# Prefix sums of a step: on GpSimd while no batch is in the pipe, on VectorE otherwise (graph message passing, one core)

## The chip, the core and the metric

The kernel runs on one core of one Trainium2 chip. The metric is the device time of one execution in microseconds (us). TensorE (PE) multiplies, its weight loads are listed as PEld, VectorE is DVE, ScalarE is ACT, GpSimd is POOL, and SyncE (SP) issues plain DMAs. GpSimd issues the indirect DMAs.

## The reference

One layer of message passing over a graph of 12,500 nodes and 800,000 edges, 64 features a node and 16 an edge, float32:

```
def reference(x, e_attr, src, dst, w_msg, w_upd):
    N, D = x.shape
    m_in = jnp.concatenate([x[src], x[dst], e_attr], axis=-1)
    msg = _silu(m_in @ w_msg)
    agg = _segment_sum(msg, dst, N)
    return _silu(jnp.concatenate([x, agg], axis=-1) @ w_upd)
```

`src` and `dst` are random, so the edges have to be sorted by target before they can be summed.

## The kernel before

The nodes are cut into 128 buckets of 98 nodes. Two streams of work run beside one another.

**Steps** sort edges. There are 782 of them. A step takes 8 columns of 128 edges. `onehot` (ScalarE, lines 394 and 395) makes `hf`, for every edge the one-hot row of its bucket. `sums` (lines 401 to 408) makes `G`, prefix sums of these rows over groups of four columns: a copy on ScalarE and two or three adds of 128x256 and 128x128 elements, in the steps of the first part of the kernel always three (403, 403, 405), each of which reads what the one before wrote. `count` (TensorE, 421 to 424) multiplies `hf` and `G` with triangular and ones matrices into `z`, from which `ranks` (VectorE, 429) takes every edge's place within its bucket. `expand` (VectorE, 438 to 442) puts the edge's record at that place in a wide row `X`, one of two buffers; its input `cb` is in PSUM. `move` (TensorE, 459) multiplies `hf` by `X`, which sends every record to its bucket's partition; ScalarE copies the result to `blk` (464, two buffers), `place` (VectorE, 477 and 478) moves the buckets' pointers on, and `scatter` (GpSimd, 482) writes the block to the store in DRAM.

**Batches** use sorted edges. A group of up to 64 tiles is formed over several periods: small VectorE work (lines 540 to 558, 588 and 589), loads of the tiles by SyncE (`rt<-st`, 564), and the conversion of the indices (525). A batch of a group is at most 8 tiles: `gather` of the source nodes' terms (GpSimd, an indirect DMA a tile, 645), one-hot rows, transposes, products, the message (677, 678), and the sum by target (694, 706).

The program is unrolled by hand: `period` writes one step and one batch in a fixed order, each at another stage of its pipe. `h` is the step that enters, `z` the one before it, `s` a block to be scattered; `q`, `t`, `a` and `r` are batches, `q` the one that enters. Each engine works through its instructions in the order in which they were written. `sums` of the entering step stands at one of two places: ahead of `expand` when a batch is in the pipe as `q`, `t` or `a`, behind `expand` when none is. A group is only formed when enough edges are sure to be sorted, by a count of steps, so that the kernel begins with 26 steps without a batch; three more come between the first groups, after which there is always a batch. In the first 20 steps the node tables are made as well (lines 193 to 209; at first four in a step, later one).

Of the kernel before, what the change touches and what calls it, by code (L numbers as in the profile page):

```python
# [7 lines left out]
OP = mybir.AluOpType  # L8
# [40 lines left out]
def mpnn_kernel(tc, x, e_attr, src, dst, w_msg, w_upd, out):  # L49
    nc = tc.nc  # L50
# [22 lines left out]
    with es:  # L73
# [303 lines left out]
        class Step:  # L377
# [16 lines left out]
                    nc.scalar.activation(c.hf[:, k, :], iof, AF.Square, bias=c.hi[:, k:k + 1])  # L394
                nc.scalar.activation(c.hf, c.hf, AF.Relu, bias=ones, scale=-1.0)  # L395

            def sums(c):

                c.G = tp.tile([P, 2, ZB, NBK], BF16, name="G")
                h = c.hf.rearrange("p (a k) b -> p a k b", k=ZB)  # L400
                nc.scalar.activation(c.G[:, :, 0, :], h[:, :, 0, :], AF.Copy)
                for k in (1, 2):
                    nc.vector.tensor_tensor(out=c.G[:, :, k, :], in0=h[:, :, 0, :] if k == 1 else c.G[:, :, k - 1, :], in1=h[:, :, k, :], op=OP.add)  # L403
                a, b = ((0, 2), (1, 2), (0, 1), (0, 1))[c.turn]
                nc.vector.tensor_tensor(out=c.G[:, a:b, 3, :], in0=c.G[:, a:b, 2, :], in1=h[:, a:b, 3, :], op=OP.add)
                if c.turn in (0, 2):
                    a = 1 if c.turn == 0 else 0
                    nc.vector.tensor_tensor(out=c.G[:, a, 3, :], in0=c.before(a), in1=c.G[:, a, 3, :], op=OP.add)

            def before(c, a):  # L410

# [299 lines left out]
        def period(step=None, batch=None, ptr_new=None):  # L711

            h, z, p, s = step, pipe["h"], pipe["z"], pipe["s"]
            q, t, a, r = batch, pipe["q"], pipe["t"], pipe["a"]
            forms = [g for g in work["forming"] if not g.ready()]
            e = None
            pipe.update(h=h, z=z, q=q, t=t, a=a)
            if q:
                q.gather(0, BT // 2)
            if s:  # L720
                s.scatter()
            if q:
                q.gather(BT // 2, BT)
            if h:
                h.onehot()
            if q:
                q.onehot()
            for g in forms:
                g.fourth()
            if z:  # L730
                z.count()
            if t:
                t.transpose(0)
                t.weights()
                t.transpose(1)
            if r:
                r.reduce()
            if z:
                z.ranks()
            if a:  # L740
                a.message()
            if r:
                r.add()
            early = q or t or a
            if h and early:
                h.sums()
            if z:
                z.expand()
            if h and not early:
                h.sums()  # L750
            if p:
                e = p.move(0)
            if t:
                t.product()
            if p:
                p.move(1)
            if e:
                e.place(ptr_new)
            for g in forms:
                g.middle()  # L760
                g.fifth()
            pipe["s"] = e
            return r
# [4 lines left out]
        class Draws:  # L768
# [34 lines left out]
            def take(d, u, units):  # L803
                for f, done in zip(d.free(u), d.done):
                    left = units
                    for b in range(NB):
                        n = min(f[b], left)
                        done[b] += n
                        left -= n
# [48 lines left out]
        def step():  # L858
            c = None
            if flow["ic"] < len(steps):  # L860
                c = next_step(flow["ic"])
                flow["ic"] += 1
            pn = None
            if pipe["z"] and pipe["z"].last:
                if flow["npl"] % 64 == 0:
                    flow["ptrs"] = sg.tile([NBK, 64], I32, name="ptrs")
                pn = flow["ptrs"][:, flow["npl"] % 64:flow["npl"] % 64 + 1]
                flow["npl"] += 1
            b = take()
            if size() and may_start() and draws.holds(state["u"], size() // state["u"]):  # L870
                draws.take(state["u"], size() // state["u"])
                g = stages[state["stage"]]
                start_group(state["u"], state["ptr"], size(), cap=g["cap"], bt=g["bt"])
            elif not size() and (not work["forming"] or work["forming"][-1].k >= 2):
                larger_from()
            if pipe["z"]:
                for i in pipe["z"].last.values():
                    draws.place(Chunk(i).m)
            period(c, b, pn)
# [35 lines left out]
        while pipe["s"]:  # L915
            period(None, take())
# [21 lines left out]
        while work["used"] < large or (work["forming"] and work["forming"][-1].k < 2):  # L938
            b = take()
            if work["used"] < large and may_start():  # L940
                start_group(QU, ptrg)
            period(None, b)
            next(upd, None)
            next(upd, None)
# [61 lines left out]
        while work["used"] < whole or lasts or work["cur"] is not None or work["forming"]:  # L1006
            b = take()
# [47 lines left out]
        with tc.If(more > 0):  # L1055
# [4 lines left out]
            with tc.If(nover > 0):  # L1060
# [27 lines left out]
                with tc.For_i(0, nover, 1):  # L1088
# [29 lines left out]
                    halves = [Step(hi[:, 0:M], rec[:, 0:M, :], 0), Step(hi[:, M:2 * M], rec[:, M:2 * M, :], 1, C - M)]  # L1118
                    for c in halves:
                        c.onehot()  # L1120
                        c.sums()
                        c.count()
                        c.ranks()

                    def block(rs=None):
                        for c in halves:
                            c.expand(rs)
                            e = c.move()
                        return e


                    c = block()
# [4 lines left out]
                    with tc.For_i(0, rounds, 1):  # L1137
                        c = block(rs)
# [36 lines left out]
```

## Time and the profile before

| | |
|---|---|
| Time before, median of 3 runs | 8929.77 us (8925.74 to 8931.5) |
| The profiled execution's own time | 8929.85 us |
| Its span in the profile | 8928.0 us |
| Busy: PE, DVE, ACT, POOL | 8156.2, 7216.6, 5054.3, 6599.6 us |
| First gather issued | 203.42 us from the span's start |

The profile shows one execution. In a row of the timeline the first number is the start in us from the span's start, then the duration, the engine, the line and the operation; what stands in brackets is the idle time of the engine before it and what ended it. In a row by line, the numbers behind the bar are the sum in us and the mean in ns, then the idle time before. TensorE's durations overlap, so starts are compared there. A row merged of several instructions has their count behind an x, and a row of the waits gives the sum of the waits in us, their number and the longest.

### The profile page before, as it was taken

Reading aid. Unit: us, or ns where it says so; the run is one execution under the profiler, and the core shown is the slowest. Engines: PE = TensorE matmul, PEld = TensorE weight load, DVE = VectorE, ACT = ScalarE, POOL = GpSimd, SP = SyncE. Lnnn points to the kernel's source line nnn. Section 1 sums busy time; section 2 is a strip of 40 time slices with the busy share of each in tenths; the row PEclk is TensorE's granted clock in tenths of the full one; section 3 lists DMA queues with packets and bytes.
Section 4 is the critical chain, followed back from the end, with each engine's and each line's share of the span. In section 5 each row is a group of like instructions: output and inputs, shape, how many; then the busy total and the mean of one; then the engine's idle time right before and its main releaser. Section 6 shows DMA issues by size and latency. Waiting matters only on the chain. (4 is left out here: it accounts for less than half of the span.)

```text
span 8928.0 us, 155380 instructions
## 1 busy us (share of the span) xinstructions
PE 8156.2 (91%) x49053; PEld 5873.2 (66%) x49816; DVE 7216.6 (81%) x15722; ACT 5054.3 (57%) x12594; POOL 6599.6 (74%) x6908
## 2 busy tenths in 40 slices
PE   8899999999999999999999999999999999999767
PEld 5677776666666666666666666666666666666656
DVE  8999998888888888888888888888888888887233
ACT  7666666555555555555555555555555555555222
POOL 1677777777777777777777777777777777777776
PEclk9999999999999999999999999999999999999566
DMA  4222222222222222222222222222222222222323
GB/s 109 56 62 60 60 61 58 50 57 54 54 56 50 57 52 56 52 56 52 56 52 56 56 52 52 55 57 52 56 52 56 52 56 55 52 57 49 59 48 51
DMA packets 662901, 501.14 MB, mean 56 GB/s; under 512 B 492983, under 2 KB 529911, under 8 KB 662071
## 3 DMA queue, kind: packets, MB, share of 16 engines
q0 software_dynamic: 238976, 349.72, 16.8%
q1 hardware_dynamic: 422775, 141.27, 7.3%
q8 instruction: 401, 6.57, 0.3%
q14 instruction: 429, 3.51, 0.1%
q10 hardware_dynamic: 320, 0.07, 0.0%
HBM read 330.05 MB, written 152.30 MB: 54 GB/s over the span
## 5 line engine op out<-in xcount | busy, mean ns | idle before, releaser
L645 POOL DMA_INDIRECT g<-A_d,sidx x6322 | 6020.1, 952 | 1946.6 <-issue 1546.2
L459 PE MATMUL pl<-X,hf 128*128 128x291 f32 (+5 forms) x12512 | 4255.3, 492 | 6.2 <-DVE LOST L477 6.2
L459 PEld LDWEIGHTS pl<-X,hf 128*128 128x128 f32 x12512 | 2389.5, 198 | 1333.1 <-issue 842.5
L442 DVE TENSOR_TENSOR X<-cb,rec 128x442 f32<-128x442 f32 (+5 forms) x3128 | 2646.9, 908 | 26.7
L394 ACT ACTIVATE hf<-iof,shi 128x128 f32<-128x128 f32 x6256 | 1908.3, 389 | 872.9 <-PE pl L459 872.6
L673 PEld LDWEIGHTS pre<-w,qt 114*128 114x128 f32 x10496 | 1338.1, 202 | 580.7 <-issue 562.8
L673 PE MATMUL pre<-w,qt 114*128 114x64 f32 x10496 | 1343.6, 284 | 249.0 <-DVE g L677 247.3
L677 DVE TENSOR_TENSOR g<-pre,g 128x512 f32<-128x512 f32 (+1 forms) x818 | 548.9, 671 | 1191.7 <-DMA g<-A_d,sidx 769.4
L678 ACT ACTIVATE g<-g 128x512 f32<-128x512 f32 (+1 forms) x818 | 501.6, 613 | 1761.5 <-DVE g L677 1759.7
L694 PE MATMUL ag<-q,g 128*64 128x98 f32 x12644 | 775.8, 264 | 250.4 <-DVE wl L549 146.1
L429 DVE TENSOR_REDUCE rank<-z 128x8 f32<-128x1024 f32 x782 | 949.1, 1214 | 57.3 <-PE z L424 36.3
L395 ACT ACTIVATE hf<-hf,ones 128x1024 f32<-128x1024 f32 x782 | 899.1, 1150 | 25.4
L667 ACT ACTIVATE qt<-tq 114x1024 f32<-114x1024 f32 (+1 forms) x818 | 797.2, 975 | 156.5 <-PE tq L664 154.2
L664 PE MATMUL tq<-ident,q 128*114 128x128 f32 x6322 | 871.5, 283 | 14.3 <-ACT nodes L194 13.0
L694 PEld LDWEIGHTS ag<-q,g 128*64 128x64 f32 x12644 | 613.3, 143 | 411.5 <-issue 200.6
L664 PEld LDWEIGHTS tq<-ident,q 128*114 128x114 f32 x6322 | 766.9, 140 | 136.5 <-ACT nodes L194 20.5
L482 POOL DMA_INDIRECT st<-blk,ptrs x567 | 572.9, 1010 | 321.2 <-issue 141.1
L655 DVE TENSOR_TENSOR q<-cb,lo 128x784 f32<-128x784 f32 (+1 forms) x818 | 767.4, 938 | 2.2
L464 ACT ACTIVATE blk<-pl 128x512 f32<-128x512 f32 (+1 forms) x568 | 323.8, 570 | 782.9 <-PE pl L459 609.7
L706 DVE TENSOR_TENSOR ACC<-ag,ACC 64x98 f32 x1938 | 497.5, 257 | 108.6 <-PE ag L694 28.8
L422 PE MATMUL z<-G,onesb 128*128 128x384 bf16 x1564 | 511.4, 327 | 73.5 <-DVE G L403 13.7
L673 PE MATMUL pre<-BW,qt 114*128 (+1 forms) x2148 | 311.8, 305 | 109.4 <-DVE g L677 108.6
(137 smaller groups left out, 5099.1 us busy)
## 6 DMA issues: line engine op xcount, KB each, us to landing
g<-A_d,sidx POOLq DMA_INDIRECT x6322
ea<-in_e_attr SPq DMA_DIRECT2D x260, 192.0 KB
rt<-st SPq DMA_DIRECT2D x1312, 34.0 KB
st<-blk,ptrs POOLq DMA_INDIRECT x567
rt<-st SPq DMA_DIRECT2D x434, 8.5 KB
nodes<-in_x SPq DMA_DIRECT2D x62, 98.0 KB
ACC<-rt SPq DMA_DIRECT2D x11, 544.0 KB
rt<-st SPq DMA_DIRECT2D x320, 17.0 KB
```

The costliest lines, as they stand in the source:

```text
L394: nc.scalar.activation(c.hf[:, k, :], iof, AF.Square, bias=c.hi[:, k:k + 1])
L395: nc.scalar.activation(c.hf, c.hf, AF.Relu, bias=ones, scale=-1.0)
L429: nc.vector.tensor_reduce(out=c.rank, in_=c.z, axis=AX.X, op=OP.max)
L442: nc.vector.tensor_tensor(out=c.x[:, k:k + 2, 2:2 + n * R].rearrange("p k (s c) -> p k s c", c=R), in0=hit[:, k:k + 2, 0:n, None].to_broad ...
L459: nc.tensor.matmul(pl[:, 0:w], c.hf[:, k, :], c.x[:, k, 0:w], start=(n == (c.size - 1 if whole else 0)), stop=ends, skip_group_check=True)
L482: i = nc.gpsimd.indirect_dma_start(out=st, out_offset=bass.IndirectOffsetOnAxis(ap=c.ptr, axis=0), in_=c.blk[:, 2:], in_offset=None)
L645: j = nc.gpsimd.indirect_dma_start(out=t.g[:, i, :], out_offset=None, in_=A_d, in_offset=bass.IndirectOffsetOnAxis(ap=t.grp.sidx[:, k:k + ...
L655: nc.vector.tensor_tensor(out=t.q[:, 0:n, 0:BK], in0=ioB[:, None, 0:BK].to_broadcast([P, n, BK]), in1=t.grp.lo[:, i0:i0 + n, None].to_broa ...
L664: nc.tensor.transpose(t.tq[0:KQ, j * P:(j + 1) * P], t.q[:, j, :], ident)
L667: nc.scalar.activation(t.qt[:, 0:w], t.tq[0:KQ, 0:w], AF.Copy)
L673: nc.tensor.matmul(t.pre[:, i * D:(i + 1) * D], t.qt[:, i * P:(i + 1) * P], w, start=True, stop=True)
L694: o = nc.tensor.matmul(t.ag[t.half(v), v // 2 * BK:(v // 2 + 1) * BK], t.g[:, i, :], t.q[:, i, 0:BK], start=(k == 0), stop=(k == u - 1))
```

## The change

`sums` gets the engine of its adds as an argument. Where it stands ahead of `expand` (a batch is in the pipe), and in the rare path at the end for overfull chunks, the adds stay on VectorE. Where it stands behind `expand` (no batch in the pipe), they are written for GpSimd.

```
-            def sums(c):
+            def sums(c, engine):
...
                 nc.scalar.activation(c.G[:, :, 0, :], h[:, :, 0, :], AF.Copy)
                 for k in (1, 2):
-                    nc.vector.tensor_tensor(out=c.G[:, :, k, :], in0=h[:, :, 0, :] if k == 1 else c.G[:, :, k - 1, :], in1=h[:, :, k, :], op=OP.add)
+                    engine.tensor_tensor(out=c.G[:, :, k, :], in0=h[:, :, 0, :] if k == 1 else c.G[:, :, k - 1, :], in1=h[:, :, k, :], op=OP.add)
                 a, b = ((0, 2), (1, 2), (0, 1), (0, 1))[c.turn]
-                nc.vector.tensor_tensor(out=c.G[:, a:b, 3, :], in0=c.G[:, a:b, 2, :], in1=h[:, a:b, 3, :], op=OP.add)
+                engine.tensor_tensor(out=c.G[:, a:b, 3, :], in0=c.G[:, a:b, 2, :], in1=h[:, a:b, 3, :], op=OP.add)
...
             early = q or t or a
             if h and early:
-                h.sums()
+                h.sums(nc.vector)
             if z:
                 z.expand()
             if h and not early:
-                h.sums()
+                h.sums(nc.gpsimd)
```

It moves 87 instructions, three in each of 29 steps. On VectorE, in the steps ahead of the first batch, before and after (`G` is the tile of prefix sums, `X` the wide row, `LOST` and `ptrs` the pointers' work):

```order
 L442 TENSOR_TENSOR X0_183<-cb_139,rec_238 128x2x357
 L442 TENSOR_TENSOR X0_183<-cb_139,rec_238 128x2x408
-L403 TENSOR_TENSOR G_323<-hf_299 128x2x128
-L403 TENSOR_TENSOR G_323<-G_323,hf_299 128x2x128
-L405 TENSOR_TENSOR G_323<-G_323,hf_299 128x128
 L273 SCALAR_TENSOR_TENSOR rec_385<-slo_234,ssi_171 128x24
 L429 TENSOR_REDUCE rank_405<-z_399 128x8
```

The three adds behind the products of `X` are gone, and the next rank follows at once. On GpSimd, at the first blocks that are scattered (`st` is the store), before:

```order
L340 MEMSET done0_153 128x1
L482 DMA st_82<-blk_427,ptr0_149 2938112x17
L482 DMA st_82<-blk_519,ptrs_388 2938112x17
L482 DMA st_82<-blk_614,ptrs_388 2938112x17
L482 DMA st_82<-blk_677,ptrs_388 2938112x17
```

and after, at the same place:

```order
L482 DMA st_82<-blk_427,ptr0_149 2938112x17
L403 TENSOR_TENSOR G_505<-hf_481 128x2x128
L403 TENSOR_TENSOR G_505<-G_505,hf_481 128x2x128
L405 TENSOR_TENSOR G_505<-G_505,hf_481 128x128
L482 DMA st_82<-blk_519,ptrs_388 2938112x17
L403 TENSOR_TENSOR G_600<-hf_576 128x2x128
L403 TENSOR_TENSOR G_600<-G_600,hf_576 128x2x128
L405 TENSOR_TENSOR G_600<-G_600,hf_576 128x128
L482 DMA st_82<-blk_614,ptrs_388 2938112x17
```

Three adds now stand between two scatters; three steps' adds stand ahead of the first scatter. TensorE's instructions keep their order; its count, of the third step here, waits for GpSimd at two places (`Pool`) where it waited for VectorE (`DVE`):

```order
L422 MATMUL z_491<-G_413,onesb_96 128x384 [waits Pool_49]
L421 LDWEIGHTS w1_94
L421 MATMUL z_491<-hf_389,w1_94 128x512
L422 LDWEIGHTS onesb_96
L422 MATMUL z_491<-G_413,onesb_96 128x384
L424 LDWEIGHTS onesb_96
L424 MATMUL z_491<-G_413,onesb_96 128x512 [waits Pool_49]
```

So the first two adds release the count's first product with `G`, and the third add releases its last one.

More of the change, by code (lines that the diff above doesn't have):

```diff
@@ L402, in sums @@
                 for k in (1, 2):
-                    nc.vector.tensor_tensor(out=c.G[:, :, k, :], in0=h[:, :, 0, :] if k == 1 else c.G[:, :, k - 1, :], in1=h[:, :, k, :], op=OP.add)
+                    engine.tensor_tensor(out=c.G[:, :, k, :], in0=h[:, :, 0, :] if k == 1 else c.G[:, :, k - 1, :], in1=h[:, :, k, :], op=OP.add)
                 a, b = ((0, 2), (1, 2), (0, 1), (0, 1))[c.turn]
-                nc.vector.tensor_tensor(out=c.G[:, a:b, 3, :], in0=c.G[:, a:b, 2, :], in1=h[:, a:b, 3, :], op=OP.add)
+                engine.tensor_tensor(out=c.G[:, a:b, 3, :], in0=c.G[:, a:b, 2, :], in1=h[:, a:b, 3, :], op=OP.add)
                 if c.turn in (0, 2):
                     a = 1 if c.turn == 0 else 0
-                    nc.vector.tensor_tensor(out=c.G[:, a, 3, :], in0=c.before(a), in1=c.G[:, a, 3, :], op=OP.add)
+                    engine.tensor_tensor(out=c.G[:, a, 3, :], in0=c.before(a), in1=c.G[:, a, 3, :], op=OP.add)
             def before(c, a):
@@ L1120, in mpnn_kernel @@
                         c.onehot()
-                        c.sums()
+                        c.sums(nc.vector)
                         c.count()
```

## The prediction

> **What bounds the kernel now.** I read the page first, for the engine that sets the long middle, then the windows of the places where no batch is in the pipe, then one period of such a place row by row.
>
> ```profile
> PE 8156.2 (91%) x49053; PEld 5873.2 (66%) x49816; DVE 7216.6 (81%) x15722; ACT 5054.3 (57%) x12594; POOL 6599.6 (74%) x6908
> L645 POOL DMA_INDIRECT g<-A_d,sidx x6322 | 6020.1, 952 | 1946.6 <-issue 1546.2
> 69.90:157.10 87.20, 84.73 (x346) 55.40 (x353) 80.95 (x172) 71.01 (x189) 13.13 (x14) 1.00 0.43 130
> 157.10:170.80 13.70, 12.00 (x53) 7.82 (x53) 13.24 (x38) 11.07 (x30) 1.92 (x2) 1.00 0.23 64
> 203.40:295.00 91.60, 74.87 (x469) 56.21 (x479) 83.28 (x213) 54.99 (x132) 69.64 (x73) 0.95 0.22 51
> 328.80:4000.00 3671.20, 3437.31 (x20816) 2463.85 (x21170) 3183.79 (x7132) 2204.16 (x5519) 2786.75 (x2902) 0.97 0.24 56
> 204.70 0.96 POOL L645 DMA_INDIRECT g<-A_d,sidx  x1 [0.30 <-issue]
> ```
>
> The columns of a window are its length and the busy time of PE, PEld, DVE, ACT and POOL. GpSimd looks 74% busy, but each gather takes 0.95 us and 0.30 us of issue after it. From the first gather to 295 us, 73 instructions at 1.25 us make 91 of 91.6 us, and from 328.8 to 4000 us 2902 of them make 3630 of 3671 us. The middle is GpSimd's queue of gathers. So the kernel is a prologue up to the first gather, a gap from 295 to 328.8 us in which no gathers are at hand, and otherwise a rigid queue: what either place gains or loses moves the end by as much. The moved sums lie in just these two places: 26 steps ahead of the first gather and 3 in the gap.
>
> One period of the prologue (start, duration, engine, line, wait before it):
>
> ```profile
> 108.46 0.96 POOL L482 DMA_INDIRECT st<-blk,ptrs  x1 [5.66 <-ACT nodes L194]
> 108.98 0.29 DVE L405 TENSOR_TENSOR G<-G,hf 128x128 bf16<-128x128 bf16 x1
> 109.00 0.34 PE L422 MATMUL z<-G,onesb 128*128 128x384 bf16 x1
> 109.17 0.39 PE L421 MATMUL z<-hf,w 128*128 128x512 bf16 x1
> 109.40 0.32 PE L422 MATMUL z<-G,onesb 128*128 128x384 bf16 x1
> 109.78 4.48 PE L459 MATMUL pl<-X,hf 128*128 128x410 f32 x16
> 109.98 1.23 DVE L429 TENSOR_REDUCE rank<-z 128x8 f32<-128x1024 f32 x1 [0.38 <-PE z L424]
> 111.72 1.15 ACT L395 ACTIVATE hf<-hf,ones 128x1024 f32<-128x1024 f32 x1
> 111.76 3.01 DVE L442 TENSOR_TENSOR X<-cb,rec 128x442 f32<-128x442 f32 x4
> 114.29 0.51 ACT L464 ACTIVATE blk<-pl 128x410 f32<-128x410 f32 x1 [0.98 <-PE pl L459]
> 114.69 0.41 DVE L403 TENSOR_TENSOR G<-hf 128x256 bf16<-128x256 f32 x1
> 115.13 0.39 PE L421 MATMUL z<-hf,w 128*128 128x512 bf16 x1
> 115.14 0.42 DVE L403 TENSOR_TENSOR G<-G,hf 128x256 bf16<-128x256 bf16 x1
> 115.62 0.34 PE L422 MATMUL z<-G,onesb 128*128 128x384 bf16 x1
> ```
>
> The cycle is 115.62 - 109.00 = 6.62 us, and it runs through VectorE: rank, products of X, first two sums, then TensorE's count (L422), and the next rank. The sums' input hf is ready at 111.72 + 1.15 = 112.87, but they wait for the products until 114.69. TensorE is nearly full as well. Where it does not wait, L422 follows L421 by 0.23 us (109.17 to 109.40); where it waits for the sums, by 0.49 us (115.13 to 115.62). So TensorE loses only 0.26 us here.
>
> **Part 1: the prologue's 13 periods with tables.** Up to 63 us, four tables a step and a late load of edge data set the pace, and I count nothing there.
>
> ```profile
> L429 DVE TENSOR_REDUCE rank<-z x13: 1215/1224/1226, 69.9 to 150.0; 128x8 f32<-128x1024 f32 x13
> PEld L422 <- DVE G L403: 8.5, 13, 1.0
> 157.11 1.22 DVE L429 TENSOR_REDUCE rank<-z 128x8 f32<-128x1024 f32 x1
> ```
>
> Thirteen periods take 157.11 - 69.91 = 87.2 us, 6.71 each with the steps that also prepare a segment. All that the count waits for the sums, seen at the weight loads, is 8.5 us; the matmul spacing above gives 13 x 0.26 = 3.4 us of it back. With the sums off VectorE three things can be last:
> - TensorE: 6.62 - 0.26 = 6.36 us.
> - VectorE: its work without the sums, 80.95 - 13 x (0.41 + 0.42 + 0.29) = 66.4 us, 5.1 a period. It is off the path.
> - A loop over two periods through the new place: ScalarE's copy of blk (107.67, one period before 114.29) to hf ready 112.87, 5.2 us; the first two sums on GpSimd, S; count to the moves 0.78 (109.00 to 109.78); moves to the next copy 4.51 (109.78 to 114.29). That is 10.5 + S, and 0.15 more on average for the edge records, so 5.3 + S/2 a period.
>
> The price S is in no row. The nearest rows are VectorE's own sums (two starts 0.45 apart, 0.87 us for both) and GpSimd's gathers (two at 1.25 = 2.5 us). GpSimd's fill of the same size is a third row:
>
> ```profile
> L321 POOL MEMSET wab<- 128x256 f32 x1 | 0.3, 301 | 0.0
> ```
>
> A fill is one stream, a sum two in and one out, so I take 3 x 0.3 = 0.9 us and 0.1 us for the hand-off: S = 2.0, nearer to the gathers' end. The loop then needs 6.3 us, just hidden under TensorE's 6.36, and I take 6.40. The part gives 87.2 - 13 x 6.40 = 4.0 us. With S = 0.87 nothing but TensorE is left; with S = 2.5 the period is 6.55 and the gain 2.0 us.
>
> The Trainium skill, "GPSIMD Engine Reference", section 3.1, speaks against the move: a two-input elementwise operation is about twice as slow there, 4497 against 2293 ns for 2048 elements. By that rule the two sums would take 1.96 x 0.83 = 1.6 us, an estimate from that page, the loop would be 6.1 us and the sum the same, as TensorE hides it; no run here shows it yet.
>
> **Part 2: two periods without tables, up to the first loads of a group.**
>
> ```profile
> 170.42 0.23 DVE L589 CAST rb<-ps 1x96 int32<-1x96 f32 x1
> 171.53 9.12 SPq L564 DMA_DIRECT2D rt<-st  x16
> 182.36 18.88 SPq L564 DMA_DIRECT2D rt<-st  x32
> 202.93 0.22 DVE L525 CAST sidx<-rt 128x64 int32<-128x64 f32 x1 [5.71 <-DMA rt<-st]
> 203.42 0.97 POOL L645 DMA_INDIRECT g<-A_d,sidx  x1 [13.35 <-DVE sidx L525]
> ```
>
> These periods take 13.7 us. The first still has a table on TensorE (6.4 us). The second is VectorE's: 13.24 us of work in both, less 2 x 1.12 of sums, is 5.5 a period, and with its waits I take 6.0. Gain 1.3 us. Here it ends: L589 lets SyncE start 48 loads, which it issues without a pause from 171.5 to 201.2 us, and the first gather follows them. What the steps between gain only lengthens VectorE's 5.71 us wait at L525. So the first gather comes 4.0 + 1.3 = 5.3 us earlier.
>
> **Part 3: the gap.**
>
> ```profile
> 308.90 3.01 DVE L442 TENSOR_TENSOR X<-cb,rec 128x442 f32<-128x442 f32 x4
> 310.29 0.39 PE L421 MATMUL z<-hf,w 128*128 128x512 bf16 x1
> 312.75 0.35 PE L422 MATMUL z<-G,onesb 128*128 128x384 bf16 x1 [2.08 <-DVE G L403]
> 313.36 1.15 ACT L395 ACTIVATE hf<-hf,ones 128x1024 f32<-128x1024 f32 x1
> 319.95 0.34 PE L422 MATMUL z<-G,onesb 128*128 128x384 bf16 x1
> 327.85 0.21 DVE L525 CAST sidx<-rt 128x64 int32<-128x64 f32 x1 [0.15 <-issue]
> ```
>
> Here the loads have landed and the gathers wait for VectorE to reach L525. The first count would not wait (2.2 us earlier, 310.29 + 0.23 against 312.75), as its hf is long ready. The second has hf at 314.5 and, with S = 2.0, its sums at 316.5 instead of 319.95. VectorE ends the first products at 311.9; 0.4 for the pointers and two rounds of 5.5 put L525 at 323.3, 4.5 us earlier. I take 4.2, and 3.5 with S = 2.5.
>
> **What else moves.** The scatter (L482) of a period now queues behind the three sums, some 3 us from 112.87, so it starts near 116 instead of 115.1. Nobody waits for it within the period: its blk has two buffers. The sums wait behind the scatter before them, which starts at 108.46 and is done ahead of hf. ScalarE's next hf also waits for GpSimd to have read the old one, three steps back. The last sums stand ahead of the first gather, but GpSimd idles 13.35 us there.
>
> Sum: 4.0 + 1.3 + 4.2 = 9.5 us, from the profiled execution's 8929.85 to 8920.3. The median of the runs, 8929.77, is the same for this purpose. A difference under 0.2% (17.9 us) is about what a measurement of this kernel cannot tell from none.
>
> **The rivals.**
> - *Slower: the sums on GpSimd are the bound.* If two dependent sums with their hand-off take S = 6 us, the loop is 5.3 + 3 = 8.3 us, 13 x 1.6 = +21 us, some 2 more in part 2, and the gap gives nothing back: 8953. It decides from S = 2.8 in part 1 and passes +0.2% near S = 5.6. Against it: six times VectorE's price. Chance 0.06.
> - *Slower: the products of X and the sums exclude one another.* Then the sums start behind L442 as now, and the cycle is today's with 2.0 in place of 0.87 us: 15 periods and 3 steps in the gap x 1.13 = +20 us, 8950. Against it: L442's first input, cb, is in PSUM. The Trainium skill, "SBUF — State Buffer", section "Who interferes with whom", has this exclusion only for a VectorE instruction with two SBUF inputs; no run here shows it yet. Chance 0.04.
> - *Faster: TensorE is not the bound, S is small.* With S = 0.87 the loop is 5.8 us: 13 x 0.93 = 12.1, part 2 gives 2.4, the gap 4.8: 8910.5. Against it: TensorE's 84.73 busy of 87.2 us. Chance 0.08.
> - *Only the gap gains*, because the first gather hangs on loads at a fixed time: 8925.6. For it: the earlier stall on edge data. Chance 0.12.
>
> That the sums are not moved is no rival: the order shows 87 instructions on the other queue.
>
> **How the numbers follow.** The forecast keeps 0.70, with its own range 8916 to 8926. Faster by over 0.2% is the third rival, 0.08; slower the first two, 0.10; the rest, 0.82, is within. The range reaches down to the third rival, 8911, and up to 8931, above the forecast with S = 3.5, where part 1 loses 4.5 us and the rest gives some 3 back; the two slow rivals stay out.
>
> **What would show it.** Right: L403 on GpSimd at 0.8 to 1 us each, periods of 6.4 us between 70 and 157 us with L422 no longer waiting, the first gather near 198 us, L525's wait for loads near 11 us, the gap's L525 some 9.5 us earlier than 327.85. Wrong: PE or PEld waiting for L403 on GpSimd for over 0.5 us a period, a first gather after 203.4, or GpSimd no longer back to back behind it.

## The result, and the profile after

| | before | after |
|---|---|---|
| Time, median of 6 runs each | 8929.59 us (8925.74 to 8932.23) | 8971.2 us (8967.81 to 8972.43) |
| Span of the profiled execution | 8928.0 us | 8969.3 us |
| First gather; first gather behind the gap | 203.42; 328.84 us | 199.96; 320.44 us |

The ratio is 1.0045, 95% interval [1.0034, 1.0055]: the change makes the kernel 41.6 us slower, where 9.5 us less was forecast. Yet in the two places that the prediction worked out, the kernel did become faster. One period of the prologue after the change (start, duration, engine, line, wait before it):

```profile
106.20 1.15 ACT L395 ACTIVATE hf<-hf,ones 128x1024 f32<-128x1024 f32 x1
106.50 2.48 DVE L442 TENSOR_TENSOR X<-cb,rec 128x578 f32<-128x578 f32 x3
107.44 0.72 POOL L403 TENSOR_TENSOR G<-hf 128x256 bf16<-128x256 f32 x1 [2.66 <-ACT hf L395]
108.24 0.68 POOL L403 TENSOR_TENSOR G<-G,hf 128x256 bf16<-128x256 bf16 x1
108.99 0.43 POOL L405 TENSOR_TENSOR G<-G,hf 128x128 bf16<-128x128 bf16 x1
109.33 0.39 PE L421 MATMUL z<-hf,w 128*128 128x512 bf16 x1
109.55 0.32 PE L422 MATMUL z<-G,onesb 128*128 128x384 bf16 x1
109.73 0.98 POOL L482 DMA_INDIRECT st<-blk,ptrs  x1 [0.31 <-PE abp L198]
115.90 0.71 PE L422 MATMUL z<-G,onesb 128*128 128x384 bf16 x2
```

GpSimd starts 0.09 us behind `hf` and needs 108.92 - 107.44 = 1.5 us for the first two adds, while VectorE is still at the products of `X`. L422 follows L421 by 0.22 us, so TensorE no longer waits, and the period is 115.90 - 109.55 = 6.35 us in place of 6.62. Next, the first loads of a group, the wait of L525 for them, and the two first gathers, from the timeline of the changed kernel:

```profile
166.83 0.23 DVE L589 CAST rb<-ps 1x96 int32<-1x96 f32 x1
167.93 9.12 SPq L564 DMA_DIRECT2D rt<-st  x16
199.47 0.21 DVE L525 CAST sidx<-rt 128x64 int32<-128x64 f32 x1 [9.93 <-DMA rt<-st]
199.96 0.98 POOL L645 DMA_INDIRECT g<-A_d,sidx  x1 [11.16 <-DMA ea<-in_e_attr]
319.95 0.21 DVE L525 CAST sidx<-rt 128x64 int32<-128x64 f32 x1
320.44 0.98 POOL L645 DMA_INDIRECT g<-A_d,sidx  x1 [0.97 <-DVE sidx L525]
```

The first gather behind the gap before the change, and the window from 328.8 to 4000 us after it (its length, then the busy time of PE, PEld, DVE, ACT and POOL):

```profile
328.84 0.97 POOL L645 DMA_INDIRECT g<-A_d,sidx  x1 [7.36 <-PE z L424]
328.80:4000.00 3671.20, 3429.91 (x20728) 2452.53 (x21080) 3165.64 (x7085) 2195.59 (x5497) 2791.95 (x2886) 0.97 0.24 56
```

The loads start 3.6 us earlier (171.53 before), the first gather 3.5 us, the first gather behind the gap 8.4 us. From there on GpSimd is back to back as before, but in the same 3671.2 us it gets through 2886 instructions in place of 2902. The groups by line of GpSimd, the scatters before the change first, then three groups after it:

```profile
L482 POOL DMA_INDIRECT st<-blk,ptrs x567 | 572.9, 1010 | 321.2 <-issue 141.1 <-ACT nodes L194 105.0 <-ACT blk L464 41.5
```

```profile
L645 POOL DMA_INDIRECT g<-A_d,sidx x6322 | 6071.8, 960 | 1937.9 <-issue 1518.9 <-DMA g<-A_d,sidx 258.4 <-PE ag L694 53.0
L482 POOL DMA_INDIRECT st<-blk,ptrs x567 | 571.5, 1008 | 185.7 <-issue 148.1 <-ACT blk L464 5.6 <-PE z L422 5.2
L403 POOL TENSOR_TENSOR G<-hf 128x256 bf16<-128x256 f32 x29 | 20.9, 722 | 108.1 <-ACT hf L395 108.1
```

The same 6322 gathers are busy for 6071.8 us where they took 6020.1. The line's own view, of before and then of after, gives the shortest, the median and the longest duration in ns, then the first and the last start:

```profile
L645 POOL DMA_INDIRECT g<-A_d,sidx x6322: 940/944/1342, 203.4 to 8906.5; - x198
```

```profile
L645 POOL DMA_INDIRECT g<-A_d,sidx x6322: 947/952/1388, 200.0 to 8947.9; - x198
```

The median has moved by 8 ns and the shortest by 7. It is so in the stretches that were read apart (328 to 1000, 4000 to 4500, 8000 to 8600 us: 944 and 952 ns in each), thousands of us behind the last moved add. The sum comes out: +51.7 us of gathers, -1.4 us of scatters (572.9 before, 571.5 after), -8.4 us in the prologue and the gap, together +41.9 us, against 41.3 us between the spans. So the loss is some 8 ns on each of 6322 instructions that the change doesn't touch. The experiments ask where these 8 ns come from.

### The profile page after: what moved, and what is told of

Its sections match the earlier page's. It is cut to its first block, busy times and chain, and to the rows that moved or that the text cites. A ratio compares the mean times of both kernels' runs of the same rounds, so it can differ in the third digit from the quotient of the medians.

```text
span 8969.3 us, 155439 instructions
## 1 busy us (share of the span) xinstructions
PE 8157.6 (91%) x49053; PEld 5865.4 (65%) x49816; DVE 7195.6 (80%) x15635; ACT 5057.0 (56%) x12594; POOL 6702.8 (75%) x6995
## 5 line engine op out<-in xcount | busy, mean ns | idle before, releaser
L645 POOL DMA_INDIRECT g<-A_d,sidx x6322 | 6071.8, 960 | 1937.9 <-issue 1518.9
L459 PE MATMUL pl<-X,hf 128*128 128x291 f32 (+5 forms) x12512 | 4266.9, 493 | 8.3 <-DVE LOST L477 8.2
L459 PEld LDWEIGHTS pl<-X,hf 128*128 128x128 f32 x12512 | 2394.1, 198 | 1341.0 <-issue 849.7
L482 POOL DMA_INDIRECT st<-blk,ptrs x567 | 571.5, 1008 | 185.7 <-issue 148.1
L422 PE MATMUL z<-G,onesb 128*128 128x384 bf16 x1564 | 512.4, 328 | 62.5 <-issue 10.5
```

The lines of the kernel that those rows point to most:

```text
L459: nc.tensor.matmul(pl[:, 0:w], c.hf[:, k, :], c.x[:, k, 0:w], start=(n == (c.size - 1 if whole else 0)), stop=ends, skip_group_check=True)
L482: i = nc.gpsimd.indirect_dma_start(out=st, out_offset=bass.IndirectOffsetOnAxis(ap=c.ptr, axis=0), in_=c.blk[:, 2:], in_offset=None)
L645: j = nc.gpsimd.indirect_dma_start(out=t.g[:, i, :], out_offset=None, in_=A_d, in_offset=bass.IndirectOffsetOnAxis(ap=t.grp.sidx[:, k:k + ...
```

## The experiments

**A single add.** Is it something that the GpSimd adds leave behind, a cost that grows with their number, or the earlier start? Three kernels are the kernel before with one add into an unused tile on GpSimd; a fourth takes VectorE's sums out of the loop in another way, without GpSimd. In this and the next code cuts, lines that only make unused tiles and counters are partly left out.

```
+        scr = cp.tile([P, NBK], BF16, name="scr")
+        nc.gpsimd.tensor_tensor(out=scr, in0=iof, in1=iof, op=OP.add)
         # e1: behind the opening fills; e2: in step 400; e3: behind the last gather
```

> The kernel before, with one unused 128x128 add on GpSimd among the fills at the start; all sums stay on VectorE. In the changed kernel the gathers take 952 ns (median) instead of 944, from the first to the last. Lasting state (one add of this kind leaves GpSimd slower for every gather behind it): gathers at 952 ns, 6322 x 8 ns = +51 us, about 8981 us. Count (each of the 87 adds costs its share): 944 ns, within 2 us of 8929.6. Shift (the earlier first gather puts the gathers at a worse phase against the other engines): 944 ns, no change, as nothing starts earlier.

> The kernel before, with the one unused add written into step 400 of 782, in the midst of the gathers. Lasting state: 944 ns up to about 4500 us, 952 ns behind it, about +25 us (8955). Presence in the program (code laid out or loaded in another way): 952 ns from the first gather on, +51 us. Count and shift: 944 ns throughout, 8930.

> The kernel before, with the one unused add behind the last gather. Presence in the program: 952 ns from the first gather on, +51 us. Lasting state, count and shift: 944 ns, 8930 within 2 us.

The fourth, in `expand` and `period`:

```
+                    if k == 2 and between:
+                        between()
...
-                z.expand()
-            if h and not early:
+                z.expand(between=h.sums if h and not early else None)
+            elif h and not early:
                 h.sums()
```

> The kernel before, with the sums of the 29 steps still on VectorE, but written between the second and the third product of X instead of behind the fourth, so that TensorE's count finds them earlier; GpSimd makes none. This starts the first gather earlier without an add on GpSimd. Lasting state, count and presence: gathers stay at 944 ns and the earlier start is kept, some 3 to 6 us before 203.4 us for the first gather and 8921 to 8926 us in all. Shift: with the first gather earlier by 3 us or more the gathers slow down as in the changed kernel, 8950 or more.

These four ran on a chip on which everything took 21% longer (kernel before: 10824.75 us) and GpSimd stood idle ahead of the gathers for 3661.0 us in e1 (1946.6 in the kernel before on the first chip). Its queue is not the bound there, so only the gathers' durations are read from these runs. Median gather: e1 952 ns, e2 944, e3 952, e4 944. e1's row of all gathers, then e2's ahead of its add and behind it, and e3's first ones:

```profile
L647 POOL DMA_INDIRECT g<-A_d,sidx x6322: 946/952/1325, 205.1 to 10761.3; - x198
```

```profile
L646 POOL DMA_INDIRECT g<-A_d,sidx x684: 938/944/1336, 1199.5 to 2399.3; - x171
...
L646 POOL DMA_INDIRECT g<-A_d,sidx x1843: 938/944/1079, 5999.4 to 8999.9; - x185
```

```profile
L646 POOL DMA_INDIRECT g<-A_d,sidx x476: 946/952/1306, 205.3 to 1198.8; - x159
```

One add is enough for all 8 ns, so it isn't their number. e3 is slow from its first gather, although its only add runs behind the last one. And e2's add, at 4955 us, changes nothing on either side of it. Any theory by which an add just slows what follows falls with e2; any by which only this run's earlier instructions count falls with e3. The totals of this chip do not show a loss: ratios of 0.9983 [0.9973, 0.9993] for e1, 1.0001 [0.9991, 1.0010] for e2, 0.9976 [0.9966, 0.9986] for e3. So here the two kernels with the longer gathers were even 0.2% faster, and no run shows why. e4, meant to show the prologue's gain without GpSimd, has its first gather at 206.1 us, not ahead of e1 to e3 (204.0 to 205.1), and a ratio of 1.0005 [0.9996, 1.0014]: no gain seen, and on this chip inconclusive, as it isn't seen there whether the end would follow.

**The program, or a draw?** Nothing in e2 and e3 differs but the add's place. So perhaps the 8 ns are drawn when a program is loaded. The changed kernel, the kernel before, e2's and e3's ran once more, unaltered, on another chip.

> The changed kernel once more, not a letter different. Theory P (the 8 ns belong to the program: something in what is built decides whether a gather takes 944 or 952 ns): median gather 952 ns again, first gather about 200 us, and where GpSimd's queue bounds the kernel the total is 40 us over the kernel before. Theory L (the 8 ns are drawn when a program is loaded and stay until it is loaded again, so the comparison of the two kernels compared two draws): 944 and 952 are both possible whatever was seen before; at 944 the total would be about 8 us under the kernel before (first gather 3.5 and the gap's first gather 8.4 us earlier, nothing later).

> The kernel before once more, not a letter different, for a profile on the same chip. Theory P: median gather 944 ns again. Theory L: 944 or 952, and a total that goes with it by 6322 x 8 ns = 51 us less what the rest of the loop hides, where GpSimd's queue bounds it. Its first gather at 203 us or, where the chip is slower, later.

> The kernel before with one unused 128x128 GpSimd add in step 400, once more; it had 944 ns per gather in its first run. Theory P: 944 again. Theory L: 944 or 952.

> The kernel before with one unused 128x128 GpSimd add behind the last gather, once more; it had 952 ns per gather in its first run although its add comes after all gathers. Theory P: 952 again. Theory L: 944 or 952.

Each kept its value: 952, 944, 944 and 952 ns. The rows of r3 and of r4:

```profile
L646 POOL DMA_INDIRECT g<-A_d,sidx x6322: 940/944/1331, 206.2 to 8908.7; - x198
```

```profile
L646 POOL DMA_INDIRECT g<-A_d,sidx x6322: 947/952/1318, 204.3 to 8959.0; - x198
```

This chip is like the first, and here the 8 ns show in the time:

| | median | ratio to before (8932.75 us) |
|---|---|---|
| r2, before again | 8932.5 us | 0.9999 [0.9988, 1.0010] |
| r3, one add in step 400 | 8932.35 us | 1.0000 [0.9989, 1.0011] |
| r4, one add behind the last gather | 8982.7 us | 1.0057 [1.0034, 1.0080] |
| r1, the changed kernel again | 8970.6 us | 1.0041 [1.0021, 1.0061] |

So the 8 ns belong to the program. A single unused add of 0.41 us, which nobody waits for, costs 50 us:

```profile
8957.78 0.95 POOL L646 DMA_INDIRECT g<-A_d,sidx  x1 [0.30 <-issue]
8959.04 0.95 POOL L646 DMA_INDIRECT g<-A_d,sidx  x1 [0.30 <-issue]
8960.01 0.41 POOL L1054 TENSOR_TENSOR scr<-iof 128x128 bf16<-128x128 f32 x1
```

The changed kernel pays the same and is 12.1 us faster than that one. That is about the gain that was forecast, seen between two kernels with gathers of equal median length; the scatters are part of it (570.7 us in r1, 576.1 in r4).

The scatters pay too, which their -1.4 us above hides: their mean is 1016 ns in r4 and 1008 in r3. GpSimd's other work does not: the first sum takes 722 ns in the changed kernel and 721 in g4 below, whose gathers are short, and the fill of L321 takes 301 ns in both. Nor does it go with how much is fetched for the program: the two instruction queues moved 401 and 429 packets in r3 and in r4 alike.

**Next to what?** In the slow kernels an add has the opening fills and iotas of a run beside it without an indirect DMA between: behind them in e1 and the changed kernel, ahead of the next run's in e3. In e2 it lies between two indirect DMAs. One theory (S) was that any fill and any add between the same two indirect DMAs do it. Four kernels: a fill and an add in step 400; the add 22 gathers ahead of the end; and the changed kernel with its first three steps' sums, those ahead of the first scatter, left on VectorE, once with the fills of the node tile on VectorE as well, once without.

```
 g1   +            if flow["ic"] == 400:
      +                nc.gpsimd.memset(scr, 0.0)
      +                nc.gpsimd.tensor_tensor(out=scr, in0=iof, in1=iof, op=OP.add)
 g6   +                    if len(ngather) == 6300:
      +                        nc.gpsimd.tensor_tensor(out=scr, in0=iof, in1=iof, op=OP.add)
 g4   -                h.sums(nc.gpsimd)
      +                nsum.append(h)
      +                h.sums(nc.gpsimd if len(nsum) > 3 else nc.vector)
 g3   as g4, and
      -                    nc.gpsimd.memset(t.xs[:, nf, :], 0.0)
      +                    nc.vector.memset(t.xs[:, nf, :], 0.0)
```

> The kernel before; in step 400 GpSimd fills an unused tile with zeros and adds into it, one behind the other (the add alone, at the same place, left the gathers at 944 ns and the time at that of before). Theory S (what counts is the order of kinds of work on GpSimd, from one run into the next: a gather turns 8 ns slower, and stays so, once a fill and an add have both run since the indirect DMA ahead of it): median gather 952 ns behind step 400 at the latest, and if the state outlasts a run 952 ns from the first gather on; total then 50 us over the kernel before, or 25 us if only the second half is slow. Theory B (only adds ahead of the first gather or behind the last one count): 944 ns throughout, total within 5 us of the kernel before.

> The kernel before with one unused GpSimd add 22 gathers ahead of the end (the same add behind the last gather made every gather of the run 952 ns). Theory S: gathers lie between this add and the fills with which the next run starts, so 944 ns throughout and a total within 5 us of the kernel before. A rival (an add near the end of the run counts, whatever lies behind it): 952 ns and 50 us over the kernel before.

> The changed kernel, but the first three steps' sums, which lie ahead of the first scatter, and the two fills of the nodes tile stay on VectorE, so that no fill and add lie between the same two indirect DMAs on GpSimd. Theory S: median gather 944 ns, first gather within 2 us of the changed kernel's 199.9, the gap's first gather within 2 us of its 321.4, and so a total of the changed kernel's 8970.6 less 50 us: 8921 us, 12 us under the kernel before and about what was forecast for the change. Theory B (adds ahead of the gathers count): 952 ns, 8971 us.

> As the one before, but the two fills of the nodes tile stay on GpSimd: the first of them comes at about 134 us between a step's sums and its scatter. Theory S: a fill and an add lie between the same two scatters, so 952 ns and 8971 us. A rival (only the adds ahead of the first scatter, behind the fills at the start, count): 944 ns and 8921 us.

All four have gathers of 944 ns (median). g1: 8930.52 us, 0.9999 [0.9989, 1.0009]; g6: 8931.19, 1.0001 [0.9991, 1.0011]; g3: 8920.97, 0.9989 [0.9979, 0.9998]; g4: 8920.53, 0.9988 [0.9978, 0.9998]. Theory S is refuted by g1 and by g4, in which a fill still lies between a step's adds and its scatter. What is left is the opening of the run. The row of g6 (compare r4's above), and that of g4:

```profile
L650 POOL DMA_INDIRECT g<-A_d,sidx x6322: 940/944/1323, 204.6 to 8906.3; - x198
```

```profile
L646 POOL DMA_INDIRECT g<-A_d,sidx x6322: 940/944/1323, 198.7 to 8898.3; - x198
```

g4 keeps 78 of the 87 moved adds and has neither the 8 ns nor the loss; its first gathers, from its timeline:

```profile
198.71 0.98 POOL L646 DMA_INDIRECT g<-A_d,sidx  x1 [11.30 <-DMA ea<-in_e_attr]
318.78 0.98 POOL L646 DMA_INDIRECT g<-A_d,sidx  x1 [0.98 <-DVE sidx L526]
```

It is 9.8 us faster than the kernel before on its chip, with 9.5 us forecast for the change. And g6 against r4 is the add moved by 22 gathers: 8931.19 us against 8982.7.

**An indirect DMA between, and the kinds in mid-run.** g4 leaves two readings: the adds must not stand next to the opening, or they must not run in the first 34 us. The next kernel is the changed one with all its adds and one unused gather of 128 rows behind the opening fills. Two more put an iota and an add, and an iota, a fill and an add, into step 400 of the kernel before.

```
 h2   +        scr = cp.tile([P, D], F32, name="scr")
      +        nc.gpsimd.indirect_dma_start(out=scr, out_offset=None, in_=x,
      +            in_offset=bass.IndirectOffsetOnAxis(ap=ip_i[:, 0:1], axis=0))
 h1   +                nc.gpsimd.iota(iscr, pattern=[[1, 1]], base=0, channel_multiplier=1)
      +                nc.gpsimd.tensor_tensor(out=scr, in0=iof[:, 0:56], in1=iof[:, 0:56], op=OP.add)
 h3   as h1, with nc.gpsimd.memset(scr, 0.0) between the two
```

> The kernel before; in step 400 GpSimd makes an index with iota and adds, one behind the other, both unused. The opening of a run on GpSimd is twelve fills and iotas, and an add next to it (ahead of the first scatter, or behind the last gather of the run before) made all gathers 952 ns; a fill and an add in step 400 did not. Theory I (iota and add between the same two indirect DMAs do it, anywhere): 952 ns behind step 400 at the latest. Theory O (only next to the opening of a run): 944 ns throughout and a time within 5 us of the kernel before.

> The same with iota, fill and add in step 400, all three kinds of the opening. Theory T (three kinds of work between the same two indirect DMAs do it, anywhere): 952 ns behind step 400 at the latest. Theory O (only next to the opening of a run): 944 ns throughout.

> The changed kernel with its 29 steps of GpSimd sums, and one unused gather of 128 rows behind the opening fills, so that an indirect DMA lies between them and the first add. Theory N (the gathers turn slower where adds run next to the opening fills, with no indirect DMA between): median gather 944 ns and a total of 8921 us, 50 us under the changed kernel's 8970.6. A rival (adds in the first 34 us make the gathers slower, whatever lies between): 952 ns and 8971 us.

On this chip all three have gathers of 947 ns, which neither theory had named; in h1 and h3 they are 947 ns ahead of step 400 and behind it. The kernel before has no profile on this chip, but its 8950.76 us (8947.94 to 8954.36) are 17 to 21 us over those of the first chip and of three others, as 3 ns on each gather would make them, so 947 ns is taken as this chip's 944. h1 took 8955.57 us and h3 8953.8 us, one run each: no 50 us, so the same kinds in mid-run did not do it. h2 took 8925.44 us, 0.9972 [0.9960, 0.9984]: not the 1.0045 of the changed kernel, but a larger gain than forecast. To set the three versions side by side, they went to one chip once more.

> The changed kernel unaltered, so that it, the one with the gather behind the fills and the one with the first three steps on VectorE stand on one chip. Theory N: its gathers are 8 ns longer than those of the other two, and its time is some 50 us over theirs and 40 us over the kernel before.

> The changed kernel with one unused gather behind the opening fills. Theory N: gathers as in the kernel before (944 ns, or what this chip has), and a time about 10 us under the kernel before (ratio 0.9989), as the one with later adds has. A rival (the 25 us of its first run, with scatters of 992 ns in place of 1024, were its own and not that chip's): a ratio near 0.997 again, with scatters some 30 ns shorter than those of the kernel with later adds.

> The changed kernel with the first three steps' sums on VectorE, for the comparison with the one before on the same chip. Theory N: gathers as in the kernel before and a ratio of 0.9988 again. The rival of the run before: 15 us longer than that one.

| | median gather | median time | ratio to before (8934.16 us) |
|---|---|---|---|
| s1, the changed kernel | 952 ns | 8971.79 us | 1.0043 [1.0027, 1.0059] |
| s2, a gather behind the fills | 945 ns | 8911.35 us | 0.9974 [0.9964, 0.9984] |
| s3, first three steps on VectorE | 945 ns | 8923.75 us | 0.9987 [0.9978, 0.9997] |

One unused gather of 1.1 us at the start takes 60.4 us off the changed kernel. Of GpSimd's groups, s1, s2 and s3:

```profile
L645 POOL DMA_INDIRECT g<-A_d,sidx x6322 | 6076.5, 961 | 1939.2 <-issue 1522.8 <-DMA g<-A_d,sidx 262.5 <-PE ag L694 49.1
L482 POOL DMA_INDIRECT st<-blk,ptrs x567 | 572.2, 1009 | 185.7 <-issue 146.3 <-ACT g L678 5.8 <-PE z L422 5.5
```

```profile
L647 POOL DMA_INDIRECT g<-A_d,sidx x6322 | 6022.3, 953 | 1938.5 <-issue 1548.2 <-DMA g<-A_d,sidx 237.7 <-PE ag L696 49.7
L484 POOL DMA_INDIRECT st<-blk,ptrs x567 | 559.4, 987 | 185.5 <-issue 145.6 <-ACT G L403 5.2 <-PE z L424 5.2
...
L342 POOL DMA_INDIRECT scr<-in_x,ip_i x1 | 1.1, 1108 | 0.2 <-issue 0.2
```

```profile
L646 POOL DMA_INDIRECT g<-A_d,sidx x6322 | 6029.8, 954 | 1938.6 <-issue 1533.2 <-DMA g<-A_d,sidx 251.7 <-PE ag L695 52.1
L483 POOL DMA_INDIRECT st<-blk,ptrs x567 | 567.4, 1001 | 185.6 <-issue 146.0 <-ACT blk L465 5.4 <-PE z L423 5.0
```

Between s1 and s2 the gathers give back 54.2 us and the scatters 12.8 us, together 67.0 us of 66.6 between the two spans (8974.5 and 8907.9 us). s2 beats both original kernels, by 22.8 us the one before. Against s3 its scatters are 14 ns shorter (8.0 us in all) and its gathers 1 ns (7.5 us): the extra gain came back on a second chip, so it belongs to the kernel, though the scatters differ by less than the 30 ns which that rival had named.

**What is shown and what is open.** Shown: the changed kernel loses its gain by these 8 ns. They are there when GpSimd adds lie between a run's opening fills and its first indirect DMA (e1 and the changed kernel), and gone, with the 50 us, when the adds start behind the first scatter (g4, s3) or a gather is put between (s2). Argued only: that the add behind the last gather (e3, r4) counts because the next run's fills follow it. It rests on one kernel, on two chips; an effect of its place at the end of the program would look the same. Open: what in GpSimd this is. No run shows why the order at the start sets the length of every indirect DMA until the end, or why a gather as the first indirect DMA shortens the scatters too. That gather was not tried in the kernel before, nor behind the adds, so it may count by being first and not by standing between. Which of the opening's instructions it takes was not tried.

## Why the prediction was wrong, point by point

**The step that failed** is the first: "otherwise a rigid queue: what either place gains or loses moves the end by as much". The queue is rigid, and both places moved the end as said. But the prediction took its pitch, 0.95 us and 0.30 us of issue, as a constant of the gather, and so put the change's effect on the 6322 gathers at nothing without giving a reason. They took 51.7 us more (median 952 ns in place of 944), by what ran on GpSimd at the start. With 6322 gathers end to end, 1 ns on each is worth 6.3 us. The working bounded the price of the adds where they stand, 26 steps and 3, and none of its cases had a price for what follows. "GpSimd no longer back to back" was named as a sign of failure; it stayed back to back, at a longer beat.

**Part 1** was sized well. Thirteen periods between the rank at 72.46 us and the one at 154.94 us take 82.5 us, 6.35 each, TensorE's floor of 6.36; 4.7 us gained against 4.0. The two sums took 1.5 us, inside the bounds of 0.87 to 2.5 and under the 2.0 taken. The estimate of 1.6 us that the prediction made from the Trainium skill, "GPSIMD Engine Reference", section 3.1, is borne out by the trace; the page's factor of about two for a two-input operation is 1.8 here for the first sum (0.72 against VectorE's 0.41 us) and 1.6 for the second (0.68 against 0.42).

**The steps ahead of it**, where nothing was counted, came 2.6 us later (72.46 against 69.91 us). Only 0.3 us of it is the late load of edge data, which ScalarE's L272 waits for (it starts at 56.47 and 56.75 us). The rest lies in the step behind it, before and then after:

```profile
61.49 0.50 PE L422 MATMUL z<-G,onesb 128*128 128x384 bf16 x1 [0.34 <-DVE G L403]
62.95 4.89 PE L459 MATMUL pl<-X,hf 128*128 128x410 f32 x16
```

```profile
62.42 0.48 PE L422 MATMUL z<-G,onesb 128*128 128x384 bf16 x1 [1.20 <-POOL G L403]
63.87 6.52 PE L459 MATMUL pl<-X,hf 128*128 128x410 f32 x16
```

There the count does wait for GpSimd's slower sums: from the end of `hf` to L422 it takes 0.66 us more. And the moves of `X` (L459) took 1.6 us longer, at a granted clock of 0.50 from 64 to 68 us, where the kernel before had 1.00. This second part differs between executions of either kernel: the same moves took 6.02 us in r2 and 5.15 in r1. On their chip the rank started at 71.68 us before the change (r2) and 72.00 after it (r1). There the first gather came 5.4 us earlier (205.3 and 199.9 us) and the one behind the gap 9.6 us (330.94 and 321.37), close to the 5.3 and 9.5 that were forecast.

**Part 2** gave 13.66 - 12.11 = 1.55 us against 1.3. (The prediction has SyncE issue its 48 loads without a pause; between the 16th and the 17th it issues two loads of indices, from 180.75 to 181.59 us.) Together the first gather came 3.5 us earlier on the first chip, not 5.3, and L525 waited 9.93 us for its loads, near the 11 expected.

**Part 3** gave 4.4 us against 4.2 at the gap's L525 (7.9 us earlier, less the 3.5). The gather behind it gained 0.5 us more, 8.4 - 3.5 = 4.9.

**The rivals.** The sums on GpSimd were not the bound, and the products of `X` and the sums ran beside one another (106.50 and 107.44 us above): both slower rivals failed on their mechanism, and what made the kernel slower was on no list. With the gathers' length held, the forecast of -9.5 us stands at -9.8 us (g4, which keeps three steps' sums on VectorE; its interval is -2 to -20 us) and, between two kernels with slow gathers, -12.1 us (r1 against r4). The working of the two places was right, and the sign of the total was not.

## What to carry to other kernels

Where one kind of instruction fills an engine's queue, its duration is a term of the sum: multiply a change of 1 ns by the count before calling anything outside of it free, and after a change compare the shortest and the median duration of that kind first. When GpSimd gets a new kind of work in a kernel that lives on its indirect DMAs, look at what stands between the opening fills and the first indirect DMA; here one unused gather there took 60 us off the changed kernel.

## What the runs showed of the hardware that was not expected

- The length of GpSimd's indirect DMAs has levels that a program keeps from chip to chip: median gathers of 944 or 952 ns (947 in three kernels on one chip, 945 and 952 on another), which followed the order of kinds of work around the start of a run. Scatters move with them (means of 1008 in r3 and 1016 in r4), adds and fills do not.
- One unused add of 0.41 us behind the last gather lengthened the run by 50 us (r4), the same add 22 gathers earlier by nothing that was seen (g6).
- The first indirect DMA of a run is longer: the first scatter took 1147 to 1152 ns, but 994 and 997 ns where a gather ran ahead of it (s2, h2), which itself took 1108 and 1112 ns.
- Chips differ too: the kernel before took 8929.6 to 8950.8 us in five sets of runs and 10824.75 us in one.
